# Retention followed by a squared-ReLU FFN: from chunk 10 on, one group of retention products per chunk, with the running state made one chunk ahead

## The chip, the cores and the metric

The kernel runs on one core of a Trainium2 chip. The metric is the device time of one execution in microseconds. A core has TensorE for matrix products (PE in the profile, and PEld for its weight loads), VectorE (DVE), ScalarE (ACT), GpSimd (POOL) and SyncE (SP), which here only issues DMAs. Each engine has its own instruction stream and takes it in order. Between engines, one waits for another by a semaphore.

## The reference, cut to what matters

```
# q, k, v: [8 batches, 8 heads, 576 positions, 64]
scores = q @ k.T / sqrt(64)
ret    = scores * where(i >= j, gamma_h ** (i - j), 0)      # gamma_h = 1 - 2**(-5-h)
attn   = ret @ v                                            # per batch and head
x      = attn.transpose(0, 2, 1, 3).reshape(4608, 512)      # tokens x model width
h      = maximum(x @ w_in, 0)                               # w_in  512 x 2048
out    = (h * h) @ w_out                                    # w_out 2048 x 512
```

The two FFN weights come as 64-bit floats and are turned into 32-bit floats on the chip.

## The kernel before, in words

**Retention.** A sequence of 576 positions is cut into chunks of 128 and a last one of 64: `ci` is 0 to 4 in a batch, and chunk 5b+4 is the half chunk. There are 40 chunks. Because the decay is a power, it can be split over q and v: GpSimd scales q (`scale_q`, L375) and v (L452, in `scores`) by tables, and the rest is linear attention. A chunk is worked in row halves of 64 positions. For each half there are three products per head:

- scores, k times q (L442, into `sc_ps`), which VectorE masks (L450) into `ret`;
- own, the half's v times its masked scores (L464, into `x_ps`);
- from the state, the running sum u of earlier k times v, times q (L499, also into `x_ps`).

A fourth, grow (L467, into `u_ps`), adds the half's k times v to the sum. ScalarE copies `u_ps` to one of three `u_sb` tiles (`grown`, L473), and `x_ps` to the FFN's input `xT` (L521).

All are products of 64x64 tiles. A product takes its contraction from 64 of the 128 rows of the array (a row half) and writes 64 of 128 output partitions (a column half), so four can stand in the array side by side. A product of 32-bit floats is two instructions in the trace. `own` has the row half of the position half h; `grow` is emitted beside it with the other row half; scores and products from the state take their row half from the head's parity `e`. Two products from different row halves that add to the same place of `x_ps` have to be kept apart: `retain_b` ends with a copy of two columns of `x_ps` by ScalarE (L502), and the products of `retain_c` wait for it.

**The FFN.** Blocks of 512 tokens are multiplied by a Strassen-like scheme of seven products a to g (`ffn_in`, L621, j = 0 to 6 below written a..g) for each of four groups `mp`. So a block takes 28 FFN steps of eight matmuls, into three rotating PSUM banks (`ps_f`). After product a ScalarE copies the bank (L631). After d ScalarE applies ReLU (L637) and GpSimd squares (L638). After the others VectorE adds, and squares (L628 and its neighbours). The first block goes another way (`first_in`, L585). A second phase, from about 560 us on, multiplies by `w_out` (L928) and has nothing of retention in it.

**The order.** It is written out by hand, and every engine's stream follows the program. In iteration i the loop emits for i > 4: `retain_a(i-1)` (own of half 1 beside grow of half 0, then `grown`), `ffn(i-1, 0)`, `retain_b(i-1)` (products from the state), `scores(i)`, `retain_c(i-1)` (own of half 0 beside grow of half 1, then the copy to `xT`), `ffn(i-1, 1)`. A half chunk has no `retain_a` products. I call each unbroken run of retention products on TensorE a visit: A for `retain_a`, BC for the rest. `ffn` emits as many FFN steps as a pacing table (`PACE`) allows for the tokens that have gone by, one to six a call. When a chunk crosses a block's border, `retain_c` first copies the part before the border, then emits FFN steps until block n-2 is finished (forced steps), and then copies the rest.

From chunk 11 on (`N_TURN`), q and k are transposed by VectorE in 32x32 tiles (`flip`, L395, two instructions a chunk) and ScalarE moves the tiles into place (`move`, L410: 16 copies for a full chunk, 8 for a half one). `ffn` takes some moves ahead of every step, and `move(C, i)` takes what is left of chunk i. The conversion of `w_out` goes in small items between the FFN steps (`w_out_parts`). One kind of item is VectorE's (L210, L214), and two activations of ScalarE (L218, L219) follow it. `held` keeps the items with ScalarE work out of the last two steps before a BC visit.

```
            retain_a(i - 1)
            if i < N_TURN:
                turn(i)
            move(C, i)
            ffn(i - 1, 0)
            retain_b(i - 1)
            if i < N_CH:
                scores(i)
            retain_c(i - 1)
            if N_TURN <= i + 2 < N_CH:
                flip(i + 2)
            ffn(i - 1, 1)
```

Of the kernel before, what the change touches and what calls it, by code (L numbers as in the profile page):

```python
# [9 lines left out]
F32 = mybir.dt.float32  # L10
# [5 lines left out]
C = 128  # L16
CH = C // 2
# [23 lines left out]
def kernel(  # L41
# [33 lines left out]
    nc = tc.nc  # L75
    ctx.enter_context(tc.manual_schedule())

    B, H, S, D = q.shape
# [242 lines left out]
            f and f()  # L321

    dv = only.tile([128, H, 2 * NCH], F32, name="dv")
    exp_bias = const.tile([128, 1], F32, name="exp_bias")
    nc.gpsimd.memset(exp_bias, -896.0 * 2.0 ** 23)
    idle, ident = (W[6][:, at:at + 128] for at in (2688, 2816))
# [30 lines left out]
    def rows(half, n=64):  # L357
        return slice(64 * half, 64 * half + n)
# [19 lines left out]


    N_TURN = 11  # L380
    moves = []

    def new_qk(i):
# [23 lines left out]
    def move(count, i=N_CH):  # L407

        while moves and count and moves[0][0] <= i and (moves[0][1] <= done[0] or count == C):
            nc.scalar.copy(*moves.pop(0)[2:])  # L410
# [16 lines left out]
    def scores(i):  # L427

        b_, ci, c0, cs = chunks[i]
        qT, kT = st[i]["qT"], st[i]["kT"]  # L430
# [6 lines left out]
        n_h = cs // CH  # L437
        for hp in range(HP):
            for h in range(n_h):
                for e in range(2):  # L440
                    t = slice(CH * h, CH * h + CH)
                    nc.tensor.matmul(sc[e][rows(h), hp, :], lhsT=kT[rows(e), hp, t], rhs=qT[rows(e), hp, t],  # L442
                                     start=True, stop=True, skip_group_check=True)

        r = st[i]["ret"] = st[i]["kT"].rearrange("p (e a) (b t) -> p e (a b) t", e=2, b=2)
        if i < N_EARLY:
            for e in range(2):
                nc.vector.tensor_tensor(r[:cs, e, :, :], sc[e][:cs], msk[:cs, 0, :, :].to_broadcast([cs, HP, CH]), op=ALU.mult)
        else:
            nc.vector.tensor_tensor(r[:cs], both[:cs], msk[:cs].to_broadcast([cs, 2, HP, CH]), op=ALU.mult)  # L450
        vs = st[i]["vs"] = loaded[i][2]
        nc.gpsimd.tensor_tensor(vs[:cs], vs[:cs],  # L452
                                dv[:cs, :, ci:ci + 1].to_broadcast([cs, H, D]), op=ALU.mult)
# [18 lines left out]
    def grown(i, h):  # L472
        nc.scalar.copy(u_sb[(2 * chunks[i][1] + h + 1) % 3], u_ps[0])  # L473
# [30 lines left out]
    def retain_c(i):  # L504

        b_, ci, c0, cs = chunks[i]
        own, grow = within(i, 0)
        more = ci + 1 < NCH
        for j in range(0, len(own), 2):
            for f in own[j:j + 2] + (grow[j:j + 2] if more else []):  # L510
                f()
        tok = b_ * S + c0
        at = tok
        p = xp[0][:, :, 0:256].rearrange("p a (g t) -> p a g t", g=2)
        while at < tok + cs:
            n = at // TOK

            while steps and steps[0][0] <= n - 2:
                step()
            end = min(tok + cs, (n + 1) * TOK)  # L520
            nc.scalar.copy(xT[n][:, :, at - n * TOK:end - n * TOK].rearrange("p (a g) t -> p a g t", a=2),  # L521
                           p[:, :, :, at - tok:end - tok])
            if more and at == tok:
                grown(i, 1)
# [4 lines left out]
        st[i] = loaded[i] = None  # L529

# [175 lines left out]
    def ffn(i, half):  # L706

        gone[0] += chunks[max(0, min(i, N_CH - 1))][3] / 2
        if steps and steps[0][0] == 0:

            move(6)
            for f in (step, lambda: convert(6)) if half else (lambda: convert(6), step):
                f()
            if half and steps and steps[0][0] == 0:
                step()
                convert(6)
            return
        if not behind:
            behind.append((gone[0] - HALF, done[0]))
        points = behind + [p for p in PACE if p[0] > behind[0][0]]  # L720
        want = points[-1][1]
        for (x0, y0), (x1, y1) in zip(points, points[1:]):
            if gone[0] < x1:
                want = y0 + (y1 - y0) * (gone[0] - x0) / (x1 - x0)
                break
        count = max(1, int(want) - done[0])
        while steps and count:
            held[0] = half == 0 and count <= 2

            move(4 if half and len(moves) > 8 else 3 if half else 2 if count > 1 else 0)  # L730
            busy[0] = len(flips) > 0
            for f in flips[:1]:
                f()
            del flips[:1]
            step()
            count -= 1
        held[0] = busy[0] = False
# [15 lines left out]
    for i in range(N_CH + 1):  # L753
        if i <= N_EARLY:

            if i == 1:
                convert(2)
            elif i == 2:
                convert(5)
            if i >= 1:  # L760
                retain_a(i - 1)
                if i < 3:
                    warm(4, False)
                elif i == N_EARLY:
                    turn(i)
                else:
                    convert(1)
                    first_in(1, (0,))
                    convert(5)
                retain_b(i - 1)  # L770
                if i < 3:
                    warm(4, False)
                retain_c(i - 1)
            convert((0, 1, 1, 0, 0)[i])
            if i == N_EARLY:
                fetch_raw(2)
                step()
            scores(i)
            if i == 2:
                convert(5)  # L780
                first_in(0, (0,))
            elif i == 3:
                convert(1)
                first_in(2, (0,))
                convert(3)
            elif i == N_EARLY:
                convert(3)
                step()
                convert(5)
            scale_q(i + 1, nc.gpsimd)  # L790
            if i < N_EARLY:
                if i < 2:
                    warm(6, False)
                if i + 1 < N_EARLY:
                    turn(i + 1)
        else:
            if i == N_EARLY + 1:
                gone[0] = TOK
# [6 lines that stand above are left out]
            if i < N_CH:  # L805
                scores(i)
            retain_c(i - 1)
            if N_TURN <= i + 2 < N_CH:
                flip(i + 2)
            ffn(i - 1, 1)  # L810
        if i == 0:
            fetch_raw(2)
        if i < N_TURN - 1:
            load(i + 3)
        else:
            if i == N_TURN - 1:
# [262 lines left out]
```

## Time and profile before

| what | us |
|---|---|
| three timed runs | 974.66, 974.70, 975.62 |
| their median | 974.7 |
| profiled execution: its span, first to last instruction | 974.5 |
| PE busy in it | 953.6 (98%) |
| DVE busy | 778.5 (80%) |
| ACT busy | 341.8 (35%) |
| POOL busy | 128.9 (13%) |
| stretch of the retention from chunk 10 on, 118.4 to 520.5 | 402.1 |
| in it: PE, DVE, ACT, POOL busy | 396.7, 334.7, 252.4, 94.3 |

The profiled execution has no other time than its span; it lies 0.2 us below the median of the timed runs. A busy PE is one with a product in flight, and products overlap, so that PE at 98% says that it seldom stood still, not that it worked at its peak. ScalarE's 35% is an average over the run: in the stretch of the retention it is 63%, and after it little. In an answer of the timeline a row is: start in us, duration, engine, line, operation, output<-inputs, shapes, how many were merged, and in brackets how long the engine had been idle and what it waited for.

### The profile page before, as it was taken

Reading aid. Unit: us, or ns where it says so; the run is one execution under the profiler, and the core shown is the slowest. Engines: PE = TensorE matmul, PEld = TensorE weight load, DVE = VectorE, ACT = ScalarE, POOL = GpSimd, SP = SyncE. Lnnn points to the kernel's source line nnn. Section 1 sums busy time; section 2 is a strip of 40 time slices with the busy share of each in tenths; the row PEclk is TensorE's granted clock in tenths of the full one; section 3 lists DMA queues with packets and bytes.
Section 4 is the critical chain, followed back from the end, with each engine's and each line's share of the span. In section 5 each row is a group of like instructions: output and inputs, shape, how many; then the busy total and the mean of one; then the engine's idle time right before and its main releaser. Section 6 shows DMA issues by size and latency. Waiting matters only on the chain.

```text
span 974.5 us, 24019 instructions
## 1 busy us (share of the span) xinstructions
PE 953.6 (98%) x10108; PEld 851.7 (87%) x10108; DVE 778.5 (80%) x1447; ACT 341.8 (35%) x848; POOL 128.9 (13%) x121
## 2 busy tenths in 40 slices
PE   6899999999999999999999999999999999999998
PEld 6645788888878888888888899999999999999998
DVE  3889799787797887888776587787888788787876
ACT  2554384864764857756631000000000000000000
POOL 3221223312222221222110000000000000000000
PEclk7999999999999999999999999999999999999999
DMA  9975756657738766487147986545353454524241
GB/s 203 245 205 160 186 161 164 184 168 242 217 93 262 207 192 188 121 279 211 62 166 274 396 309 249 191 157 184 109 205 141 160 198 171 208 100 173 88 174 44
DMA packets 172011, 181.43 MB, mean 186 GB/s; under 512 B 118144, under 2 KB 132480, under 8 KB 165248
## 3 DMA queue, kind: packets, MB, share of 16 engines
q1 hardware_dynamic: 169792, 179.38, 58.1%
q8 instruction: 79, 1.29, 0.6%
q10 hardware_dynamic: 2112, 0.52, 0.3%
q14 instruction: 28, 0.23, 0.1%
HBM read 109.36 MB, written 70.52 MB: 185 GB/s over the span
## 4 chain that ended last, share of the span: by engine, by line
PE 92%; DVE 3%; ACT 2%; DMA 2%; issue 1%; SPq 0%; DVEq 0%
PE h_b L621 17%; PE o_b L928 17%; PE h_a L621 11%; PE h_c L621 11%; PE o_a L928 11%; PE o_c L928 11%; PE h_ps L585 4%; PE x_ps L464 3%; PE x_ps L499 2%; PE sc_ps L442 2%; DMA g<-g_dram 1%; PE u_ps L467 1%; DVE w L225 1%; DVE w L228 1%; PE t_ps L421 0%
## 5 line engine op out<-in xcount | busy, mean ns | idle before, releaser
L621 PE MATMUL h_b<-room,w 128*128 128x256 f32 x768 | 185.7, 385 | 1.9 <-DVE room L548 1.9
L410 ACT COPY qk<-flip 32x256 f32<-32x256 f32 x416 | 167.4, 402 | 11.3 <-DVE flip L395 5.4
L621 PEld LDWEIGHTS h_b<-room,w 128*128 128x128 f32 x768 | 143.8, 190 | 22.9 <-issue 2.0
L928 PE MATMUL o_b<-w,room 128*128 128x128 f32 x1168 | 144.4, 275 | 0.2 <-DVE room L880 0.2
L928 PEld LDWEIGHTS o_b<-w,room 128*128 128x128 f32 x1168 | 137.3, 192 | 0.4 <-DVE room L880 0.4
L928 PE MATMUL o_c<-w,room 128*128 128x128 f32 x1008 | 123.0, 275 | 0.0
L621 PE MATMUL h_c<-room,w 128*128 128x256 f32 x512 | 122.8, 383 | 0.0
L621 PE MATMUL h_a<-room,w 128*128 128x256 f32 x512 | 122.5, 382 | 0.0
L928 PEld LDWEIGHTS o_c<-w,room 128*128 128x128 f32 x1008 | 117.7, 192 | 0.0
L942 ACT COPY r<-o_a 128x128 f32<-128x128 f32 x53 | 14.1, 265 | 272.3 <-PE o_a L928 236.6
L621 PEld LDWEIGHTS h_c<-room,w 128*128 128x128 f32 x512 | 97.0, 191 | 13.7
L621 PEld LDWEIGHTS h_a<-room,w 128*128 128x128 f32 x512 | 96.0, 190 | 13.9 <-issue 0.5
L928 PE MATMUL o_a<-w,a 128*128 128x128 f32 x688 | 85.6, 275 | 0.0
L928 PEld LDWEIGHTS o_a<-w,a 128*128 128x128 f32 x688 | 81.2, 192 | 0.1
L638 POOL TENSOR_TENSOR room<-room 128x512 f32<-128x512 f32 x32 | 35.0, 1094 | 347.0 <-ACT room L637 294.2
L628 DVE SCALAR_TENSOR_TENSOR room<-room 128x512 f32<-128x512 f32 x96 | 73.7, 767 | 3.3
L585 PE MATMUL h_ps<-room,w 128*128 128x512 f32 (+1 forms) x152 | 58.9, 535 | 2.9 <-DVE w L228 2.2
L640 DVE TENSOR_TENSOR room<-h_b,room 128x512 f32<-128x512 f32 x32 | 22.1, 690 | 49.5 <-PE h_b L621 49.5
L375 POOL TENSOR_TENSOR q_ld<-q_ld,dv 128x512 f32<-128x512 f32 (+1 forms) x39 | 45.9, 1177 | 83.5 <-DMA q_ld<-in_q_dram 65.2
L464 PEld LDWEIGHTS x_ps<-qk,v_ld 64*64 64x64 f32 x1152 | 40.3, 136 | 16.7 <-issue 13.2
L464 PE MATMUL x_ps<-qk,v_ld 64*64 64x64 f32 x1152 | 49.6, 226 | 4.0 <-ACT u_sb L502 2.0
L452 POOL TENSOR_TENSOR v_ld<-v_ld,dv 128x512 f32<-128x512 f32 (+1 forms) x40 | 48.9, 1224 | 12.6 <-DMA v_ld<-in_v_dram 12.6
(104 smaller groups left out, 1335.3 us busy)
## 6 DMA issues: line engine op xcount, KB each, us to landing
g_dram<-room SPq DMA_DIRECT2D x32, 1280.0 KB, 5.7
a<-g_dram SPq DMA_DIRECT2D x30, 1024.0 KB, 5.8
room<-g_dram SPq DMA_DIRECT2D x15, 1024.0 KB, 5.8
w<-w_dram SPq DMA_DIRECT2D x7, 1792.0 KB, 15.3
out_dram<-room SPq DMA_DIRECT2D x17, 512.0 KB, 3.3
w<-in_moe_w_in_dram SPq DMA_DIRECT2D x16, 512.0 KB, 5.3
w<-in_moe_w_out_dram SPq DMA_DIRECT2D x16, 512.0 KB, 4.3
v_ld<-in_v_dram SPq DMA_DIRECT2D x31, 256.0 KB, 4.0
```

Source lines behind the costliest of these rows:

```text
L375: engine.tensor_tensor(t, t, dv[:cs, :, NCH + ci:NCH + ci + 1].to_broadcast([cs, H, D]), op=ALU.mult)
L410: nc.scalar.copy(*moves.pop(0)[2:])
L442: nc.tensor.matmul(sc[e][rows(h), hp, :], lhsT=kT[rows(e), hp, t], rhs=qT[rows(e), hp, t], start=True, stop=True, skip_group_check=True)
L452: nc.gpsimd.tensor_tensor(vs[:cs], vs[:cs], dv[:cs, :, ci:ci + 1].to_broadcast([cs, H, D]), op=ALU.mult)
L464: own.append(lambda hp=hp, e=e, b=b: nc.tensor.matmul(x_at(hp, b, h), lhsT=s["vs"][rows(h), 2 * hp + b, :], rhs=s["ret"][rows(h), e, hp, : ...
L499: nc.tensor.matmul(x_at(hp, b, h), lhsT=u[rows(e), hp, :], rhs=s["qT"][rows(e), hp, CH * h:CH * h + CH], start=clears(b, hp // 2), stop=Fa ...
L585: nc.tensor.matmul(p.rearrange("p h t -> p (h t)"), lhsT=w[:, c, :], rhs=xT[0][:, c, lo * HT:hi * HT], start=(c == 0), stop=(c == N_DM - 1))
L621: nc.tensor.matmul(p[:, mm, :], lhsT=w[:, c, :], rhs=xs[n][right][:, c, :], start=(j in OPENS and mm == 0 and c == 0), stop=(j in CLOSES a ...
L628: nc.vector.scalar_tensor_tensor(t, t, 0.0, t, op0=ALU.max, op1=ALU.mult)
L638: nc.gpsimd.tensor_tensor(g["A11"], g["A11"], g["A11"], op=ALU.mult)
L640: nc.vector.tensor_tensor(g["A22"], p, p15, op=ALU.add)
L928: nc.tensor.matmul(p, lhsT=s["lefts"][left][:, m, :], rhs=w_out[j][:, m, WO_SLOT[right], :], start=(i in OPENS and m == 0), stop=(i in CLO ...
```

## The change

From iteration 11 on, the two visits of a chunk become one, `whole(i)`, and the two calls of `ffn` become one, `ffn(i-1, 2)`, whose token count is the second half of chunk i-1 and the first half of the next, so that the pacing at the `xT` copies is the same as before. `whole(i)` emits:

1. own of half 0 beside grow of half 1; after the first half of them a copy by ScalarE of one column of a small tile (`mark`), which waits for them (`f1`); then `grown(i, 1)`;
2. scores of chunk i+1, position half 0 only;
3. products from the state for both halves; their first waits for `f1`; after their last a second small copy (`f2`), for full chunks;
4. own of half 1 beside grow of half 0 of the next chunk, first half of them;
5. scores of chunk i+1, position half 1 only, and the mask;
6. the second half of step 4; own waits for `f2`;
7. the copies to `xT`, and `grown(i+1, 0)` after the first of them.

A half chunk has no own of half 1, and in the chunk before a half chunk step 5 has no products and there is no grow for the next chunk: a half chunk has only half 0, and its state goes no further. The state for a chunk's half 1 is thus made in the visit of the chunk before it. The scaling of v for chunk i+1 (`scale_v`) moves from `scores` to the end of iteration i, after `ffn(i-1, 2)` and just ahead of `whole(i)`, whose step 4 reads it. `ffn(., 2)` takes two to four moves a step, by how many are still due for the next chunk, none in its last step; and `held` covers the last step only. Iteration 10 keeps the old visits and adds grow of half 0 of chunk 10 after them.

```diff
+    N_ONE = N_TURN - 1
...
+    def scored(i, hs):
+        if hs == (0,):
+            scores(i, True)
+        for h in hs:
+            if h < chunks[i][3] // CH:
+                for hp in range(HP):
+                    score(i, st[i]["sc"][0], hp, h)
...
+        if i < N_ONE:
+            scale_v(i)
+
+    def scale_v(i):
+        ci, cs = chunks[i][1], chunks[i][3]
         vs = st[i]["vs"] = loaded[i][2]
         nc.gpsimd.tensor_tensor(vs[:cs], vs[:cs],
                                 dv[:cs, :, ci:ci + 1].to_broadcast([cs, H, D]), op=ALU.mult)
...
+    def seen(done_):
+        a = nc.scalar.copy(mark[:, 1:2], mark[:, 0:1])
+        after(a, done_)
+        return a
...
+    def whole(i):
...
+        out_of, into = own_of(i, 0), grow_of(i, 1) if more else []
+        f1 = seen(beside_each(out_of, into, (0, 2))[-1])
+        beside_each(out_of, into, (4, 6))
+        if more:
+            grown(i, 1)
+        if i + 1 < N_CH:
+            scored(i + 1, (0,))
+        f2 = None
+        for h in range(cs // CH):
+            if 2 * ci + h == 0:
+                continue
+            u = u_sb[(2 * ci + h) % 3]
+            for hp, e, b in HEADS[0:2] + HEADS[4:6] + HEADS[2:4] + HEADS[6:8]:
+                m = nc.tensor.matmul(x_at(hp, b, h), lhsT=u[rows(e), hp, :], rhs=s["qT"][rows(e), hp, CH * h:CH * h + CH],
+                                     start=clears(b, hp // 2), stop=False, skip_group_check=True)
+                if f1:
+                    after(m, f1)
+                    f1 = None
+        if cs == C:
+            f2 = seen(m)
+        grows = i + 1 < N_CH and chunks[i + 1][3] == C
+        out_of, into = own_of(i, 1) if cs == C else [], grow_of(i + 1, 0) if grows else []
+        beside_each(out_of, into, (0, 2))
+        if i + 1 < N_CH:
+            scored(i + 1, (1,))
+            masked(i + 1)
+        last = beside_each(out_of, into, (4, 6))
+        if f2:
+            after(last[0], f2)
+        x_out(i, lambda: grown(i + 1, 0) if grows else None)
...
         gone[0] += chunks[max(0, min(i, N_CH - 1))][3] / 2
+        if half == 2:
+            gone[0] += chunks[min(i + 1, N_CH - 1)][3] / 2
...
-            held[0] = half == 0 and count <= 2
-
-            move(4 if half and len(moves) > 8 else 3 if half else 2 if count > 1 else 0)
+            held[0] = half != 1 and count <= (1 if half else 2)
+
+            if half == 2:
+                due = sum(m[0] <= i + 2 for m in moves)
+                move(max(2, min(4, -(-due // (count - 1)))) if count > 1 else 0)
+            else:
+                move(4 if half and len(moves) > 8 else 3 if half else 2 if count > 1 else 0)
...
+        elif i > N_ONE:
+            move(C, i)
+            whole(i - 1)
+            if N_TURN <= i + 2 < N_CH:
+                flip(i + 2)
+            ffn(i - 1, 2)
...
+            if i == N_ONE:
+                for f in grow_of(i, 0):
+                    f()
+                grown(i, 0)
...
+            if i == N_ONE:
+                ffn(i, 0)
...
+        if N_ONE - 1 <= i < N_CH - 1:
+            scale_v(i + 1)
```

`beside_each(own, grow, js)` emits, for each j, two of the first list and then two of the second; `after` adds a semaphore wait.

More of the change, by code (lines that the diff above doesn't have):

```diff
@@ L323 @@
     dv = only.tile([128, H, 2 * NCH], F32, name="dv")
+    mark = const.tile([128, 2], F32, name="mark")
+    nc.vector.memset(mark, 0.0)
     exp_bias = const.tile([128, 1], F32, name="exp_bias")
@@ L425, in turn, with scores @@
         nc.vector.tensor_copy(to[:, 0].rearrange("p d h t -> p h d t"), p[:, :n_h, 0, :, :])
-    def scores(i):
+    def scores(i, halves=False):
         b_, ci, c0, cs = chunks[i]
-        qT, kT = st[i]["qT"], st[i]["kT"]
         if i < N_EARLY:
@@ L436, in scores, with score, masked @@
             sc = [both[:, e, :, :] for e in range(2)]
-        n_h = cs // CH
+        st[i]["sc"] = sc if i < N_EARLY else (sc, both)
+        if halves:
+            return
         for hp in range(HP):
[L439 to L443, printed above, removed]
+            for h in range(cs // CH):
+                score(i, sc, hp, h)
+        masked(i)
+    def score(i, sc, hp, h):
+        for e in range(2):
+            t = slice(CH * h, CH * h + CH)
+            nc.tensor.matmul(sc[e][rows(h), hp, :], lhsT=st[i]["kT"][rows(e), hp, t], rhs=st[i]["qT"][rows(e), hp, t],
+                             start=True, stop=True, skip_group_check=True)
+    def scored(i, hs):
[5 more added lines that the diff above has]
+                    score(i, st[i]["sc"][0], hp, h)
+    def masked(i):
+        b_, ci, c0, cs = chunks[i]
+        sc = st[i]["sc"]
+        if i >= N_EARLY:
+            sc, both = sc
         r = st[i]["ret"] = st[i]["kT"].rearrange("p (e a) (b t) -> p e (a b) t", e=2, b=2)
@@ L511, in retain_c, with x_out @@
                 f()
+        x_out(i, lambda: grown(i, 1) if more else None)
+    def x_out(i, after):
+        b_, ci, c0, cs = chunks[i]
         tok = b_ * S + c0
@@ L522, in retain_c @@
                            p[:, :, :, at - tok:end - tok])
-            if more and at == tok:
-                grown(i, 1)
+            if at == tok:
+                after()
             at = end
@@ L529, in retain_c, with grow_of @@
         st[i] = loaded[i] = None
+    HEADS_1 = [(hp, e, e if hp < HP // 2 else 1 - e) for e in (1, 0) for hp in (0, 2, 1, 3)]
+    def grow_of(i, h):
+        ci = chunks[i][1]
+        if ci == 0 and h == 0:
+            u_ps[0] = ps_u.tile([128, HP, D], F32, tag="u", name="u_ps")
+        u = u_ps[0]
+        return [lambda hp=hp, e=e, b=b: nc.tensor.matmul(
+            u[rows(e), hp, :], lhsT=loaded[i][1][rows(h), 2 * hp + e, :], rhs=st[i]["vs"][rows(h), 2 * hp + b, :],
+            start=(ci == 0 and h == 0 and hp == 0), stop=(hp == HP - 1), skip_group_check=True) for hp, e, b in HEADS]
@@ new lines, in own_of, with after @@
+    def own_of(i, h):
+        s = st[i]
+        return [lambda hp=hp, e=e, b=b: nc.tensor.matmul(
+            x_at(hp, b, h), lhsT=s["vs"][rows(h), 2 * hp + b, :], rhs=s["ret"][rows(h), e, hp, :],
+            start=clears(b, hp // 2), stop=False, skip_group_check=True) for hp, e, b in HEADS_1]
+    def after(later, earlier):
+        tc.add_manual_dep(later.ins, earlier.ins.name,
+                          mybir.DependencyInfo(mybir.DependencyClass.Sync, mybir.DependencyReason.DATA), reason="row halves")
@@ new lines, in seen, with beside_each @@
+    def seen(done_):
+        a = nc.scalar.copy(mark[:, 1:2], mark[:, 0:1])
+        after(a, done_)
+        return a
+    def beside_each(own, grow, js):
+        made = []
+        for j in js:
+            made.extend(f() for f in own[j:j + 2] + grow[j:j + 2])
+        return made
+    def whole(i):
+        b_, ci, c0, cs = chunks[i]
+        s = st[i]
+        xp[0] = ps_x.tile([128, 2, 256], F32, tag="x", name="x_ps", padded_shape=[128, 2, 512])
+        clean.clear()
+        more = ci + 1 < NCH
+        out_of, into = own_of(i, 0), grow_of(i, 1) if more else []
[6 more added lines that the diff above has]
+        f2 = None
+        for h in range(cs // CH):
+            if 2 * ci + h == 0:
[19 more added lines that the diff above has]
+        x_out(i, lambda: grown(i + 1, 0) if grows else None)
```

## The prediction, written before the result was known

> **What bounds the kernel now.** I read the page first, then the timeline around the visits, then the clock by windows. The page's chain of work that ended last:
>
> ```profile
> PE 92%; DVE 3%; ACT 2%; DMA 2%; issue 1%; SPq 0%; DVEq 0%
> ```
>
> TensorE sets the time; DMA adds 2%. So a change is worth what it adds to or takes from TensorE's stream. The timeline around an A visit gives its price:
>
> ```profile
> 302.33 1.89 PE L621 MATMUL h_b<-room,w 128*128 128x256 f32 x8
> 304.15 0.27 PE L464 MATMUL x_ps<-qk,v_ld 64*64 64x64 f32 x2
> ...
> 304.38 0.23 PE L464 MATMUL x_ps<-qk,v_ld 64*64 64x64 f32 x2
> 304.39 0.23 PE L467 MATMUL u_ps<-v_ld,k_ld 64*64 64x64 f32 x2
> 304.43 0.23 PE L464 MATMUL x_ps<-qk,v_ld 64*64 64x64 f32 x2
> ...
> 304.78 1.99 PE L621 MATMUL h_a<-room,w 128*128 128x256 f32 x8
> 306.61 0.38 PE L621 MATMUL h_b<-room,w 128*128 128x256 f32 x1
> ```
>
> From 302.33 to 306.61, 4.28 us, lie two FFN steps and the visit. Steps without a visit between follow at 1.73 us (306.61 and 308.33), so the visit costs 0.82. Its 32 instructions go in eight rounds of four; a round takes 0.058 us (304.32, .38, .43, .49): 0.47. The other 0.36 is the price of leaving the 128x128 products and coming back. I call it the switch.
>
> How many instructions fit in a round depends on which quarters of the array they use:
>
> ```profile
> 310.61 0.56 PEld L442 LDWEIGHTS sc_ps<-qk 64*64 64x64 f32 x16
> 319.09 0.56 PEld L442 LDWEIGHTS sc_ps<-qk 64*64 64x64 f32 x32
> 319.67 0.57 PEld L464 LDWEIGHTS x_ps<-qk,v_ld 64*64 64x64 f32 x16
> ```
>
> Scores of a full chunk take 32 instructions, of a half chunk 16, and both 0.56 us: scores of one position half only use one column half, two quarters, so a round holds two. The same with a half chunk's own without grow (L464, 16 in 0.57).
>
> The third view is a BC visit that starts at 205.44, after an FFN step d:
>
> ```profile
> 205.44 0.69 PE L499 MATMUL x_ps<-qk,u_sb 64*64 64x64 f32 x32
> 205.59 0.60 ACT L637 ACTIVATE room<-h_a 128x512 f32<-128x512 f32 x1 [3.09 <-issue]
> 206.20 0.16 ACT L502 COPY u_sb<-x_ps 128x2 f32<-128x2 f32 x1
> 206.27 1.04 POOL L638 TENSOR_TENSOR room<-room 128x512 f32<-128x512 f32 x1 [11.49 <-ACT room L637]
> 207.27 1.06 POOL L452 TENSOR_TENSOR v_ld<-v_ld,dv 128x512 f32<-128x512 f32 x1
> ```
>
> d's ReLU ends 0.75 us into the visit, GpSimd's square then runs, and the scaling of v ends 2.89 us into the visit. Now that is hidden: that v is first read some FFN steps later.
>
> **What the skill says.** The Trainium skill, "TensorEngine Tiling (Array Packing)", Key Properties: changing the tiling mode drains TensorE, and different tiles run in parallel. The trace agrees: 0.36 us a switch, 7 ns from one tile's start to the next's, 58 ns until the same tile's. Its Gotcha 1: row tiles may not access one PSUM bank at once and software must order them; hence `f1` and `f2`. "TensorE: Matmul & The Clock Gate", Architectural detail: ScalarE and GpSimd are strict FIFO; the trace agrees (L452 follows L638 at once). Same page, Part 1: an idle window of about 3.4 us halves TensorE's clock. The trace has one such, at clock 0.50:
>
> ```profile
> 287.49:290.91 3.42, 1.51 (x37) 1.28 (x37) 3.39 (x6) 2.57 (x6) 0.00 (x0) 1.00 0.00 0
> 290.91:294.32 3.41, 3.41 (x10) 2.66 (x9) 2.85 (x6) 0.00 (x0) 0.00 (x0) 0.50 0.21 29
> ```
>
> TensorE was busy for 1.51 of 3.42 us, then slow for a window.
>
> **The change, part by part** (30 visits, chunks 10 to 39).
>
> *Rounds and switches.* Before: ci=1, 2: A 0.82 (8 rounds) and BC 1.80 (24 rounds 1.40, switch 0.36, some 0.04 for L502): 2.62. ci=3: the same. ci=0: 0.82 and a BC of 20 rounds: 2.45. ci=4: BC alone, 20 rounds and a wait of 0.12: 1.65. After, the scores of a full next chunk come as two halves of 8 rounds each, where both together took 8. ci=1, 2: 8+8+8+8+8 = 40 rounds, 2.33+0.36 = 2.69 (+0.06). ci=0 has half the state products: 36 rounds, 2.46 (+0.01). ci=3: no second score half, but own of half 1 is alone, 8 rounds: 32 rounds, 2.22, and a wait for `f2`. The tiny copy's loop, from the half-chunk visits: product 0.218, 0.07 until the copy, 0.16, 0.055 until the next product: 0.50. Only own's first half, 0.23, covers it: 0.27 more, 2.50 (-0.13). ci=4: own alone 8, score halves 16, state 4, grow alone 8: 36 rounds, 2.46 (+0.81): it never had an A visit to lose. Chunk 39 saves 0.31; the grow added behind chunk 9 costs 0.47. Sum: 6x0.01+12x0.06-6x0.13+5x0.81-0.31+0.47 = +4.3 us. So 24 switches (8.6 us) go and 12.9 us of half-filled rounds come. Elsewhere 12 to 16 rounds (0.7 to 0.9) lie between a tiny copy's product and its waiter: hidden if ScalarE is free.
>
> *GpSimd.* `scale_v(i+1)` stands behind d's square and ahead of the visit that reads it. Step 4's grow comes after 24 rounds, 1.45 us in. Where d is the last FFN step before the visit, the row above says that v is ready at 2.89: TensorE waits 1.49, and all behind it in its queue too. I laid the FFN steps of each interval out by the pacing table; for the kernel before it gives the runs of steps seen in the trace. d stands last, with a grow to come, before visits 15, 16, 17, 19, 22, 26, 27, 35, 36, 37. In 27 and 36 ScalarE is later still (below). 7x1.49 + 1.72 (half chunk 19, whose grow comes after 20 rounds) = 12.1; visit 25 gives 1.4 more, because d's ReLU there is stuck behind moves: 13.5. With e last, the scaling ends about 1.15 in: hidden. Ends: 0 if something lets v be scaled earlier; 18 if GpSimd runs at its slow 1.5 us.
>
> *ScalarE.* A move takes 0.402. An interval after a border has forced steps without moves, then four steps with 4+4+4+0, and four are left to be flushed in front of the visit. The kernel before shows such an interval's start:
>
> ```profile
> 469.76 0.72 ACT L218 ACTIVATE w<-w,exp_bias 128x512 uint32<-128x512 uint32 x1 [5.93 <-DVE w L210]
> 470.39 0.66 ACT L219 ACTIVATE w<-w 128x512 f32<-128x512 uint32 x1
> 470.95 0.35 ACT L521 COPY room<-x_ps 128x256 f32<-128x256 f32 x1
> 471.32 1.65 ACT L410 COPY qk<-flip 32x256 f32<-32x256 f32 x4
> 472.99 0.58 ACT L631 COPY room<-h_a 128x512 f32<-128x512 f32 x1
> ```
>
> The FFN run began at 463.07, so L631 ends at +10.5. Two times four moves, d's ReLU, four moves and `f1` bring 16.2, while TensorE wants it at 7 steps (12.4) + 0.98 = 13.35: visit 27 loses 2.9. Visit 36, without a conversion item, loses 1.5. Visit 24 (two flushed, a conversion two steps before) 0.85, visit 25 0.4, some 0.5 elsewhere: 6.2. Ends: 2, and 10 if conversion items stand right before more visits.
>
> *VectorE.* The stall at 288 (a block's sums late) loses its cover, an A visit: +0.8. The later mask is read a whole interval on: nothing, hidden by six FFN steps; without them its 0.68.
>
> *What goes.* Waits now seen: A visits at 229.7 and 471.4 behind that late L521 (0.88, 1.22; now seven FFN steps lie between), the late L502 at 180.3 (1.03), 343.9 (0.35), smaller ones 0.2: -3.7.
>
> SP's loads and the squares keep their number and order. Tiny copies: 0.16 each, in ScalarE's slack.
>
> Sum: +4.3+13.5+6.2+0.8-3.7 = +21.1. The profiled execution's 974.5 becomes 995.6; the median stood 0.2 above: 995.8.
>
> **Rivals.** (1) *Nothing is late.* GpSimd and ScalarE deliver before TensorE asks, v by 1.45 us into each visit and `f1` by 0.98. Then 19.7 falls away: 976.1, no measurable change. It decides where all lateness together stays under 0.5 us. For it: with a, b, c, f or g last, GpSimd is done early. Against: the 2.89 of the third view, met with nothing before it in GpSimd's queue. (2) *Half of it*: only one of the two queues is late, or d stands last less often: 982 to 989. (3) *The clock.* Each long stall may cost a window at half clock: 3.41 us at half speed loses 1.7. 0.44 busy tripped it; the stall at 471 (2.25 of 3.40 busy) didn't. Visits with 1.5 us of waiting stay near 0.55. If half of ten trip, and VectorE, which waits longer for scores, falls behind: 1002 to 1015. (4) *Half-filled rounds pack with their neighbours* and (1) holds as well: 974.5-8.6-3.7+0.8 = 963. Against: score halves stand between products that are in order with them.
>
> **How the numbers follow.** A measurement of this kernel can tell 0.2% (1.95 us) from no change. The likeliest case, 0.55, gives 995.8, by itself 989 to 1002. (2) 0.16, (3) 0.13, (1) 0.14 with its spread over 971 to 981: faster 0.05, same 0.05, slower 0.04. (4) 0.02, faster. So faster 0.07, same 0.05, slower 0.88. The range 979 to 1008 leaves out (4), most of (1) and half of (3).
>
> **What would show it.** Visits of 2.69 us without waits, and score halves of 16 instructions in 0.47 us each: the rounds. Grow (L467's successor) waiting for v about 1.5 us in eight visits behind d: GpSimd. Long waits for ScalarE at visits 27 and 36, with moves ahead of the tiny copy. The A stalls of 229 and 471 gone. The prediction is wrong if grow doesn't wait, or if score halves take 0.23.

## The result, and the profile after

The changed kernel takes 1007.9 us (median of four runs, 1006.8 to 1009.1) against 974.7 in the same session: a ratio of 1.034, 95% interval 1.0326 to 1.0355. It is 33.2 us slower; 21.1 were predicted. The profiled execution spans 1005.7 us against 974.5. Lines have moved: in the new listing own is L577, grow L571, the products from the state L616, scores L450, the tiny copies L586, the scaling of v L479, the moves L413, an FFN product L724.

The page after, busy time by engine, the chain that ended last, and two groups:

```profile
PE 967.6 (96%) x10108; PEld 869.9 (86%) x10108; DVE 777.5 (77%) x1448; ACT 344.9 (34%) x872; POOL 129.1 (13%) x121
...
PE 39%; DVE 1%; issue 0%; DVEq 0%
...
L472 DVE TENSOR_TENSOR qk<-sc_ps,msk 128x512 f32<-128x512 f32 (+1 forms) x36 | 24.6, 685 | 46.4 <-PE sc_ps L450 46.4
...
L571 PE MATMUL u_ps<-v_ld,k_ld 64*64 64x64 f32 x768 | 41.7, 229 | 12.1 <-POOL v_ld L479 12.1
```

PE was busy 953.6 us before and is busy 967.6 now; the other 17 of the 31 us are time in which nothing was in flight, so more than half of the loss is waiting. The last line names a wait that the kernel before did not have: grow waits 12.1 us for GpSimd's scaling of v. VectorE's mask waits 46.4 us for scores, but that is slack of VectorE: its result is wanted a whole interval later. The chain covers only the second phase this time (39% of the span) and says nothing of the retention.

Where the 31 us lie is read from the timeline, visit by visit: the time between the last FFN product before a visit and the first after it, against visits without a wait. The retention's stretch grew by 34.3 us (the part before it was some 2 us shorter in this execution):

| in the stretch of the retention | predicted | measured |
|---|---|---|
| rounds and switches | +4.3 | +4.7 |
| grow waits for GpSimd, in nine visits | +13.5 | +14.0 |
| waits for ScalarE, and what else is in the visits | +6.2 | +9.9 |
| FFN steps: sums of block 4 | +0.8 | +0.4 |
| FFN steps: k of chunk 13 arrives late | 0 | +4.0 |
| half-clock windows: four instead of one | 0 | +5.1 |
| waits of before that are gone | -3.7 | -3.9 |
| sum | +21.1 | +34.2 |

The timeline after, around visit 16, which starts at 210.24 behind an FFN step d, to be held against the third view of before:

```profile
210.24 0.27 PE L577 MATMUL x_ps<-qk,v_ld 64*64 64x64 f32 x2
...
210.40 0.60 ACT L740 ACTIVATE room<-h_a 128x512 f32<-128x512 f32 x1 [2.98 <-issue]
...
210.76 0.63 PE L450 MATMUL sc_ps<-qk 64*64 64x64 f32 x16
...
211.07 1.07 POOL L741 TENSOR_TENSOR room<-room 128x512 f32<-128x512 f32 x1 [13.23 <-ACT room L740]
...
212.10 1.05 POOL L479 TENSOR_TENSOR v_ld<-v_ld,dv 128x512 f32<-128x512 f32 x1
...
213.21 0.27 PE L571 MATMUL u_ps<-v_ld,k_ld 64*64 64x64 f32 x2 [1.13 <-POOL v_ld L479]
...
214.28 1.99 PE L724 MATMUL h_b<-room,w 128*128 128x256 f32 x8
```

ReLU, square, scaling, grow: the chain of the prediction. The scaling ends 2.91 us into the visit (2.89 predicted). From one product's start to the next (from start to start, below) TensorE loses 1.35 us here; over the nine visits it is 1.32 to 2.55, together 14.0.

The timeline after in front of visit 27, which starts at 377.37: ScalarE's queue and the product that waits for it.

```profile
374.81 0.59 ACT L734 COPY room<-h_a 128x512 f32<-128x512 f32 x1
375.42 3.33 ACT L413 COPY qk<-flip 32x256 f32<-32x256 f32 x8
...
378.77 0.60 ACT L740 ACTIVATE room<-h_a 128x512 f32<-128x512 f32 x1
379.39 1.64 ACT L413 COPY qk<-flip 32x256 f32<-32x256 f32 x4
...
381.05 0.19 ACT L586 COPY mark<-mark 128x1 f32<-128x1 f32 x1
...
381.30 0.74 PE L616 MATMUL x_ps<-qk,u_sb 64*64 64x64 f32 x32 [2.77 <-ACT mark L586]
```

Eight moves, d's ReLU, four moves, the tiny copy: the order the prediction wrote out, and 2.99 us lost from start to start for 2.9 forecast.

Two things were not in the sum. The clock, by windows after (us from the start, length, busy time and instructions of PE, PEld, DVE, ACT, POOL, then the granted clock, the DMA share, GB/s):

```profile
344.27:347.68 3.41, 1.32 (x64) 1.17 (x56) 2.65 (x3) 1.13 (x4) 2.86 (x2) 1.00 0.00 0
347.68:351.09 3.41, 3.17 (x47) 2.88 (x48) 1.31 (x2) 1.30 (x4) 1.20 (x2) 0.50 0.71 209
378.40:381.81 3.41, 0.64 (x38) 0.52 (x36) 0.03 (x1) 3.01 (x8) 2.37 (x3) 1.00 1.02 294
381.81:385.23 3.42, 3.42 (x65) 3.03 (x57) 1.31 (x2) 1.64 (x5) 0.70 (x1) 0.50 0.90 197
```

These are visits 25 and 27. After a window in which the waits left TensorE 1.32 or 0.64 us of 3.41 busy, the next runs at half clock. The windows from 262.35 and 491.04 run at half clock too, after windows with 1.91 and 1.66 us busy. Four windows that lose 1.7 us each, against one before, make +5.1.

And the loads, in the timeline after (SPq is SP issuing a DMA):

```profile
123.48 0.38 SPq L666 DMA_DIRECT2D g_dram<-room  x1
123.91 0.52 SPq L148 DMA_DIRECT2D q_ld<-in_q_dram  x1
...
127.05 0.56 SPq L148 DMA_DIRECT2D k_ld<-in_k_dram  x1
...
132.80 0.71 DVE L398 STREAM_TRANSPOSE flip<-k_ld 128x512 f32<-128x512 f32 x1 [6.19 <-DMA k_ld<-in_k_dram]
...
134.14 1.99 PE L724 MATMUL h_c<-room,w 128*128 128x256 f32 x8 [2.74 <-DVE room L738]
...
136.81 1.99 PE L724 MATMUL h_b<-room,w 128*128 128x256 f32 x8 [0.67 <-DVE room L743]
```

SP reaches the loads at 123.91, behind a store of the FFN's output that it could only issue when the data was there. VectorE's flip waits 6.19 us for the k that arrives too late, the FFN's sums stand behind the flip, and TensorE stands twice, 3.1 and 1.1 us from start to start where 0.22 is usual. With the slower start after each, the way from visit 10 to visit 11 takes 18.6 us, against 14.7 in the kernel of the second experiment below: 4.0 us. In the kernel before, the same loads go out first and the store after them:

```profile
115.97 0.39 SPq L148 DMA_DIRECT2D q_ld<-in_q_dram  x1
...
117.47 0.47 SPq L148 DMA_DIRECT2D k_ld<-in_k_dram  x1
...
127.10 0.37 SPq L563 DMA_DIRECT2D g_dram<-room  x1
```

### The profile page after: what moved, and what is told of

Its sections match the earlier page's. It is cut to its first block, busy times and chain, and to the rows that moved or that the text cites. A ratio compares the mean times of both kernels' runs of the same rounds, so it can differ in the third digit from the quotient of the medians.

```text
span 1005.7 us, 24074 instructions
## 1 busy us (share of the span) xinstructions
PE 967.6 (96%) x10108; PEld 869.9 (86%) x10108; DVE 777.5 (77%) x1448; ACT 344.9 (34%) x872; POOL 129.1 (13%) x121
## 5 line engine op out<-in xcount | busy, mean ns | idle before, releaser
L724 PE MATMUL h_b<-room,w 128*128 128x256 f32 x768 | 186.8, 387 | 2.7 <-DVE room L651 1.9
L413 ACT COPY qk<-flip 32x256 f32<-32x256 f32 x416 | 167.3, 402 | 5.5
L724 PEld LDWEIGHTS h_b<-room,w 128*128 128x128 f32 x768 | 146.8, 193 | 24.9 <-issue 2.2
L724 PE MATMUL h_c<-room,w 128*128 128x256 f32 x512 | 122.5, 382 | 2.7 <-DVE room L738 2.7
L724 PE MATMUL h_a<-room,w 128*128 128x256 f32 x512 | 122.0, 381 | 0.0
L724 PEld LDWEIGHTS h_c<-room,w 128*128 128x128 f32 x512 | 97.2, 191 | 16.7 <-DVE room L738 3.1
L724 PEld LDWEIGHTS h_a<-room,w 128*128 128x128 f32 x512 | 96.5, 190 | 14.0 <-issue 0.5
L731 DVE SCALAR_TENSOR_TENSOR room<-room 128x512 f32<-128x512 f32 x96 | 69.5, 724 | 3.3
L377 POOL TENSOR_TENSOR q_ld<-q_ld,dv 128x512 f32<-128x512 f32 (+1 forms) x39 | 49.0, 1258 | 100.1 <-DMA q_ld<-in_q_dram 85.9
L472 DVE TENSOR_TENSOR qk<-sc_ps,msk 128x512 f32<-128x512 f32 (+1 forms) x36 | 24.6, 685 | 46.4 <-PE sc_ps L450 46.4
L571 PE MATMUL u_ps<-v_ld,k_ld 64*64 64x64 f32 x768 | 41.7, 229 | 12.1 <-POOL v_ld L479 12.1
L688 PEld LDWEIGHTS h_ps<-room,w 128*128 128x128 f32 x152 | 27.6, 190 | 25.7 <-issue 21.9
```

The costliest lines, as they stand in the source:

```text
L377: engine.tensor_tensor(t, t, dv[:cs, :, NCH + ci:NCH + ci + 1].to_broadcast([cs, H, D]), op=ALU.mult)
L571: return [lambda hp=hp, e=e, b=b: nc.tensor.matmul(u[rows(e), hp, :], lhsT=loaded[i][1][rows(h), 2 * hp + e, :], rhs=st[i]["vs"][rows(h), ...
L688: nc.tensor.matmul(p.rearrange("p h t -> p (h t)"), lhsT=w[:, c, :], rhs=xT[0][:, c, lo * HT:hi * HT], start=(c == 0), stop=(c == N_DM - 1))
L724: nc.tensor.matmul(p[:, mm, :], lhsT=w[:, c, :], rhs=xs[n][right][:, c, :], start=(j in OPENS and mm == 0 and c == 0), stop=(j in CLOSES a ...
L731: nc.vector.scalar_tensor_tensor(t, t, 0.0, t, op0=ALU.max, op1=ALU.mult)
```

## The experiments

### The scaling of v taken out of the square's way

```diff
             whole(i - 1)
+            if i < N_CH - 1:
+                scale_v(i + 1)
...
-        if N_ONE - 1 <= i < N_CH - 1:
+        if N_ONE - 1 <= i <= N_ONE:
             scale_v(i + 1)
```

> The kernel after, with the scaling of v for chunk i+1 issued right after the visit of chunk i-1 instead of right before the visit of chunk i. Theory of the GpSimd queue: the nine waits of grow for v (13.7 us of gaps) vanish; three of the four windows at half clock followed such a wait (262, 348, 491 us), so up to 5 us more goes; ScalarE's waits at the same visits come out from behind them and stay. 1007.9 becomes about 990 (987 to 995). Rival, the waits come from the v loads or from GpSimd being slow: within 3 us of 1007.9. Rival, the clock has nothing to do with the waits: about 994, four slow windows remain.

Measured: 990.2 us (ratio 1.0164, interval 1.0144 to 1.0183), 17.7 less than the changed kernel. GpSimd's timeline in it:

```profile
199.62 1.06 POOL L479 TENSOR_TENSOR v_ld<-v_ld,dv 128x512 f32<-128x512 f32 x1
212.31 1.06 POOL L741 TENSOR_TENSOR room<-room 128x512 f32<-128x512 f32 x1 [11.63 <-ACT room L740]
```

v for the visit that starts at 211.5 is scaled eleven us ahead; the square at 212.31 has nothing of the retention behind it, and no grow waits for GpSimd in the whole trace. Visits behind d that wait for nothing else take 2.5 to 2.8 us. The waits for ScalarE at visits 27 (2.99) and 36 (1.75) stand as they were, so these are two independent causes, and GpSimd's is the larger: 14.0 of the 17.7 us are its waits. The windows at half clock behind them are gone, but this execution still had three in the stretch, behind the late loads, visit 13 and visit 27, so that the other 3.7 us are not traced to the clock. One wait grew: that of visit 20 for ScalarE, from 0.38 to 1.63 us.

### The loads back in front

```diff
             ffn(i - 1, 1)
-            if i == N_ONE:
-                ffn(i, 0)
...
+        if i == N_ONE:
+            ffn(i, 0)
```

The second place is behind the loads of the same iteration; nothing but SP's order changes.

> The kernel after, with the one moved call of ffn in iteration 10 put behind the loads of chunks 13 and 14 as it was before; only the order of SyncE's stream changes. Theory of the load queue: the transpose of chunk 13 no longer waits 6.2 us for its k, the two stalls in the FFN run at 124 to 140 us (3.95 us) vanish: about 1004. Rival, VectorE was late by itself there: no change.

Measured: 1004.8 us (1.0308, 1.0284 to 1.0331), 3.1 less. Its timeline:

```profile
116.00 0.47 SPq L148 DMA_DIRECT2D k_ld<-in_k_dram  x1
...
123.95 0.38 SPq L666 DMA_DIRECT2D g_dram<-room  x1
...
126.86 0.70 DVE L398 STREAM_TRANSPOSE flip<-k_ld 128x512 f32<-128x512 f32 x1
```

The loads go out ahead of the store, the flip finds its data, and of the 4.0 us of FFN stall nothing is left; the 3.1 gained agree with it within the interval.

### Moves in the forced steps

```diff
             while steps and steps[0][0] <= n - 2:
+                if i >= N_ONE:
+                    move(4)
                 step()
```

> The kernel after, with four moves ahead of each forced step at a block's border, so that nothing is flushed in front of visits 27 and 36. Theory of the ScalarE queue: the waits for the tiny copy at these two visits (3.0 and 1.75 us) and the window at half clock behind visit 27 (1.7 us) go, about 1001.5 to 1003. At visit 36 less may show, 1.5 us of GpSimd's lateness comes out from behind ScalarE's, so 1002 to 1005. Rival, moves don't matter and the conversion items hold ScalarE: no change.

Measured: 1004.2 us (1.0307, 1.0289 to 1.0324), 3.7 less. The tiny copies of visits 27 and 36 are no longer waited for. But grow in both visits now waits 1.50 us for v: both visits stand behind a d, and GpSimd's lateness had been hidden behind ScalarE's. A stall removed shows the next one, and only the difference is gained, 1.7 us; one half-clock window less (three for four in the stretch) gives about as much again.

### All three together

> The kernel after with the three edits together: v scaled right after the previous visit, the loads of chunks 13 and 14 ahead of the moved FFN steps, four moves ahead of each forced step. Theory that the waits are those of three queues and add up: 990.2 less 3 to 4 for the loads, less 4.7 for visits 27 and 36, less 1.7 to 3.4 for windows at half clock: 979 to 983. What is left over 974.4 is then rounds (4.7), the conversion item before visit 13 (1.5), waits for the tiny copy elsewhere. Rival, one wait only hides the next and they don't add: 986 or more.

Measured: 982.0 us (1.0085, 1.0068 to 1.0102), 25.9 less than the changed kernel, where the three alone give 17.7 + 3.1 + 3.7 = 24.5. The clock of its profiled execution:

```profile
core 0: 977.6 us, clock 1.000
```

In this execution no window of the retention falls to half clock: the +5.1 hang on the waits. It was the fastest of the four, 979.7 us; the others took 981.2 to 984.3 at mean clocks of 0.998, 0.996 and 0.991, and no trace shows where their half-clock windows lie. So what is left of the loss, 7.6 us by the medians, is the rounds (stall-free visits still take 2.67 us), single waits at visits 13 and 20 (1.4 each), 24 (0.7) and 35 (0.6), and a part of the clock that is not shown.

### Half-filled rounds put into the kernel before

```diff
-        for hp in range(HP):
-            for h in range(n_h):
+        for hp, h in [(hp, h) for hp in range(HP) for h in range(n_h)] if i <= N_TURN - 1 else [(hp, h) for h in range(n_h) for hp in range(HP)]:
+            for _ in range(1):
```

The kernel before with the scores of half 0 ahead of those of half 1, and nothing else.

> The kernel before, with the scores of chunks 11 to 39 in the order of the changed kernel (all heads of position half 0, then all of half 1); nothing else. 23 of these chunks are full. Theory of the half-filled rounds: 8 rounds of 0.058 us more for each, 0.47 us, 10.7 us in all, less some 0.04 us a visit in which the copy that orders row halves was waited for: 974.7 becomes 984 to 985.5. Rival, two halves pack with their neighbours: 974.7.

Measured: 977.9 us against 974.4 (1.0035, 1.0021 to 1.005): 3.5 us, a third of the forecast. The expectation failed, and the timeline of this kernel shows how; the same two rows in the kernel before follow.

```profile
410.26 0.77 PE L442 MATMUL sc_ps<-qk 64*64 64x64 f32 x26
410.81 0.27 PE L464 MATMUL x_ps<-qk,v_ld 64*64 64x64 f32 x1
410.86 0.28 PE L442 MATMUL sc_ps<-qk 64*64 64x64 f32 x3
```

```profile
281.06 0.65 PE L442 MATMUL sc_ps<-qk 64*64 64x64 f32 x32
281.53 0.27 PE L464 MATMUL x_ps<-qk,v_ld 64*64 64x64 f32 x2
```

Mixed, 32 scores take 0.47 us to the next product. Half behind half they should take 0.94; own's first product starts 0.55 in, with scores still starting after it. Half-filled rounds that stand next to each other overlap, with each other and with the products behind them, and a visit of ci=1, 2 grows by 0.25 us and one of ci=0 or 4 by 0.14 to 0.20, not by 0.47. In the changed kernel the halves stand apart, and there stall-free visits took 2.67 us where 2.69 was forecast.

### Scores split by heads instead of by halves

```diff
-        for h in hs:
-            if h < chunks[i][3] // CH:
-                for hp in range(HP):
-                    score(i, st[i]["sc"][0], hp, h)
+        for hp in (0, 1) if hs == (0,) else (2, 3):
+            for h in range(chunks[i][3] // CH):
+                score(i, st[i]["sc"][0], hp, h)
```

The same products as in the kernel with all three edits, but each of the two places now holds both position halves of two head pairs, so that a full chunk's rounds are full.

> As the run with the three edits, and the scores of the next chunk divided between their two places by head pairs instead of position halves, so that each place has all four quarters: 4 rounds in each place where there were 8. Theory of the half-filled rounds: a full visit with a full next chunk falls from 2.57 us between FFN products to about 2.10 and some 0.05 to 0.25 of waiting for the tiny copies, whose cover falls from 12 rounds to 8: 24 visits by 0.25 to 0.45, 6 to 11 us, so 970 to 976. Rival, from the run with the kernel before: TensorE overlaps half-filled rounds anyway, and 2 us or less is gained.

Measured: 978.0 us (1.0035, 1.0022 to 1.0047), 4.0 less: short of the forecast of 6 to 11, and more than the rival's 2. Stall-free visits of full chunks fall from 2.67 to 2.47 us. But eight rounds instead of twelve now lie between a tiny copy's product and its waiter, and where a or d is the last FFN step the copy comes late: in some twelve visits. There the products behind it start 0.31 us after those ahead of it instead of 0.12, and 0.2 of the gain is given back.

### Conversion items held back

```diff
-            held[0] = half != 1 and count <= (1 if half else 2)
+            held[0] = half != 1 and count <= 2
```

and, to make up for it, a pace of 1.0 instead of 0.92 and a catch-up step at j = 1.

> As the run before in this list, and conversion items with ScalarE work held out of the last two FFN steps before a visit, as the kernel before does, with the pacing of these items quickened from 0.92 to 1.0 a step so that they end in time. Theory: the wait at visit 13 (1.5 us) and small ones at 11 and 20 go, 1 to 3 us less than the run before in this list. Rival: the quicker items crowd VectorE and it is no faster.

Measured: 975.2 us against 974.4 (1.001, 1.0003 to 1.0018): all but even with the kernel before. Visits 13 and 24 lost their waits, visit 20 did not. The hold and the pace were changed together; what each gives is not shown.

### The sums of block 4, in the old kernel and in the new

Both kernels stop for 1.9 to 2.0 us in front of product b of block 4 because VectorE makes a flip and other work before the block's second sum; in the prediction's view of the clock it is the window at 287.49. The edit makes that sum right behind the first and lets the flip wait for one step:

```diff
             sums_x[n + 1].pop(0)()
+            if j == 5 and len(sums_x[n + 1]) > 2:
+                sums_x[n + 1].pop(0)()
+                late_x[0] = True
```

> The kernel before with only the second sum of a late block moved ahead of the flip, as a control for the two others: the wait of 1.9 us before product b of block 4 and its half-clock window (1.7) go, 974.4 less 3.6 is 970.8, within 970 to 972.5. If it lands there, the part of the gain of the other two that comes from this edit has nothing to do with one group of products per chunk. If the window doesn't go with the wait, 972.5.

Measured: 971.9 us against 974.5 (0.9969, 0.996 to 0.9979). The stretch around the same step, in windows:

```profile
284.00:287.41 3.41, 3.41 (x17) 3.00 (x16) 3.38 (x6) 2.25 (x6) 0.32 (x1) 1.00 0.00 0
287.41:290.82 3.41, 3.41 (x46) 2.75 (x45) 3.34 (x6) 0.96 (x2) 0.00 (x0) 1.00 0.00 0
```

No wait and no window at half clock behind it. This is the fastest kernel of the study, and it has none of the change.

> The five edits as before it, and in the last FFN steps of a block whose successor's x came late, VectorE makes the second of the block's sums (T2, which product b of the next block reads) right behind the first and ahead of a flip, and whatever is left of the weight conversion is emitted before block 7's last group. Theory: TensorE's wait of 2.0 to 2.4 us in front of product b of block 4 and the half-clock window behind it (1.7) go: 975.2 less 3.7 is 971.5, within 970.5 to 973. Rival: product g's sum, now one instruction later, holds b's bank, and 0.9 of the wait stays with the half-clock window gone: 972.5. Rival: the wait goes but the window comes elsewhere, as in all runs but one so far: 973.

Measured: 975.7 us (1.0012, 1.0003 to 1.0021), no gain. The stall at 288 went, but this kernel lacked the catch-up step at j = 1, so seven items of the weight conversion were left and were emitted at once before block 7's last group:

```profile
533.94 0.69 DVE L745 TENSOR_TENSOR room<-h_b,room 128x512 f32<-128x512 f32 x1 [6.91 <-DMA g_dram<-room]
...
534.69 2.48 PE L726 MATMUL h_b<-room,w 128*128 128x256 f32 x8 [3.21 <-DVE room L745]
```

VectorE waits there for a store of the FFN's output to land, and TensorE for VectorE. How the left-over items make that store late was not traced; the wait is gone in the kernel with the catch-up step (two runs below).

The next run is this kernel with the items held out of three steps instead of two.

> The same with the conversion items with ScalarE work kept out of the last three steps before a visit instead of two. Theory: the moves of chunk 21 no longer stand behind an item that waits 2.6 us for VectorE, and visit 20 falls from 4.0 to 2.35 us: 1.6 less than the kernel without this edit, 969.9 if that gives 971.5. Rival: the items bunch up in fewer steps, their VectorE parts delay block sums and masks elsewhere, and nothing is gained: equal within 0.5 us.

Measured: 987.6 us (1.0132, 1.0115 to 1.0149). With still more of the conversion left to the end TensorE waits there for 5 and then 7 us. Visit 20 takes 2.3 us, but so it does in the run just before, without this edit: in both, the lagging conversion puts no item in front of visit 20. So this run tells nothing of its question.

> The kernel with the five edits (catch-up steps of the weight conversion included, which the kernel before this one lacked) and the second block sum ahead of the flip; nothing of the conversion is left to be emitted in one go. In the kernel before this one that rest made TensorE wait 3.4 us at 534.7 and cost a half-clock window (1.7). Theory: both go, and 975.7 less 5.1 gives 970.6, within 969.5 to 972.5. Rival: visit 20, which fell from 4.0 to 2.2 us there only because the conversion lagged, is slow again: 972.3 or more.

Measured: 973.4 us against 974.3 (0.9996, 0.9986 to 1.0006): not to be told from the kernel before, and above the forecast. The rest's stall is gone, and the rival was right that visit 20 is slow again once the conversion keeps up, as the timeline shows:

```profile
259.93 0.72 ACT L218 ACTIVATE w<-w,exp_bias 128x512 uint32<-128x512 uint32 x1 [2.36 <-DVE w L210]
...
261.26 1.24 ACT L413 COPY qk<-flip 32x256 f32<-32x256 f32 x3
...
261.71 0.33 PE L450 MATMUL sc_ps<-qk 64*64 64x64 f32 x2 [0.58 <-ACT qk L413]
```

ScalarE stands 2.36 us at a conversion item for VectorE, the last moves of chunk 21 stand behind it, and the scores wait for them.

The last run splits the scores three head pairs to one:

```diff
-        for hp in (0, 1) if hs == (0,) else (2, 3):
+        for hp in (0, 1, 2) if hs == (0,) else (3,):
```

> The same with the scores of three head pairs in the first place and of one in the second, so that twelve rounds instead of eight lie between the tiny copy's product and its waiter. Theory: the wait of 0.31 us for the tiny copy in some twelve visits behind a or d falls to 0.1, and own's second tiny copy, now covered by 0.46 us against its 0.50, adds 0.04 to twenty visits: 1.7 less than the kernel beside it, 968.9 if that gives 970.6. Rival: the copies are late because ScalarE is, not by cover, and nothing changes: equal within 0.5.

Measured: 973.5 us (0.9993, 0.9984 to 1.0003), no gain. The step to the first waiting product falls from 0.31 to 0.19 us in the visits behind a or d, and own's second half, behind the other tiny copy, rises from 0.12 to 0.23: what one copy gains in cover the other loses. Visits of full chunks behind a or d stay at 2.67 us.

## Why the prediction was right, and where not

*Direction, and most of the amount.* Slower by 21.1 was forecast, 33.2 came. That is 0.1 us inside the upper end of the range given, 979 to 1008, and outside the 989 to 1002 of the likeliest case by itself. The range reached so far because it took in half of rival (3), while 4.0 us of what filled it, the late loads, stood in no rival: that it held is in part luck. The three large terms hold. Rounds and switches: +4.3 forecast (the line as written adds up to 4.2), +4.7 measured; in visit 12 the scores of half 0 start two every 0.058 us, 0.47 in all, as said. GpSimd: the nine visits named are the nine that wait, 13.5 against 14.0, and with the scaling moved the waits are gone; here two errors cancel, visit 25 lost 2.55 for 1.4 and the other eight 11.5 for 12.1. ScalarE: visits 27 and 36 lost 2.99 and 1.75 us for 2.9 and 1.5. Rivals (1) and (2) fall with that, (4) with the stall-free visits; the waits said to go went (3.9 for 3.7).

*The clock: the step that failed most.* Rival (3) had the mechanism and its price, but the sum took only the likeliest case and set it at zero, on the ground that visits with 1.5 us of waiting stay near 0.55 busy. Neither part of that ground held. The working itself gave visit 27 a loss of 2.9 us; and 0.55 was not known to be safe, only that 0.44 tripped the clock and 0.66 did not. Here windows busy for 1.91 and 1.66 of 3.41 us, 0.56 and 0.49, tripped it. Nor need a window be idle, as in the sentence that the prediction cites: one that is partly idle is enough. The Trainium skill, "TensorE: Matmul & The Clock Gate", Part 1, says that the window of 3413 ns runs freely, and the trace agrees: the starts of the four half-clock windows lie 25, 10 and 32 times 3.413 us apart. So it matters where a wait falls on that grid. The stall behind the late loads shows it: in the changed kernel a border of the grid splits it, 2.17 and 1.91 us busy on the two sides, and no half clock follows; in the first and third experiments the same stall leaves one window with 0.84 and 0.86 us busy, and it does. Of the twelve visits that wait for more than one us, four paid. Three are those that waited longest, 27 (2.99 us), 25 (2.55) and 35 (0.63 and 1.56), and they paid in each of the traces of the changed kernel and the first three experiments in which these waits stand. Visit 19 (1.71) paid here and not in the second experiment, visit 13 (1.58) there and not here. So the size of a wait counts first, and near 1.6 us the grid.

*SP's loads: a wrong statement.* "SP's loads and the squares keep their number and order" was wrong: the FFN steps of chunk 10's first half had been moved ahead of the loads of iteration 10, and with them the store that SP issues for the FFN. The diff showed it (`if i == N_ONE: ffn(i, 0)`); the working had followed the moved step's VectorE and ScalarE work, not its DMAs. +4.0 us, 3.1 of it regained by undoing that one move.

*ScalarE elsewhere: a term sized too small.* The 0.5 for other visits became some 3: visit 13 (1.58), where a conversion item waited 4.25 us for VectorE, then 35 (0.63), 20 (0.38) and 17 (0.36). That is the upper end named, where conversion items stand right before more visits; the sum had taken the middle. About 1.5 us more of that row lies in the visits that wait for GpSimd, which take some 0.2 us longer than their wait explains; why is open.

*What the structure is worth.* With whole rounds, stall-free visits save 0.15 to 0.17 us in each of 24 chunks with two visits before and cost 0.43 in each of five half chunks: 24 x 0.16 - 5 x 0.43 = 1.7 us gained. The 0.2 that the exposed tiny copies take back in twelve visits is 2.4, more than all of it. A visit of 32 full rounds and one switch should take 2.23 us, and took 2.47. The other 0.24 are the tiny copies again: at each of the two the trace has a step of 0.12 and then one of 0.09 us where 0.04 is usual, 0.13 a copy. No run here leaves the copies out. No version of it tried here beat the old order with its one stall mended.

## What to carry to other kernels

Joining two groups of products saves a switch, but moves every input's deadline forward by an interval: for each input, write down which engine makes it and what that engine has in its queue ahead of it at that moment. For a step that is moved, do this for its DMAs also. Add up the waits last, against windows of the clock, since a wait of 1.6 us can cost 3.3.

## What the hardware showed that was not expected

- Half-clock windows lie on a fixed grid of 3.413 us. Of the windows on this grid from 120 us on that ran at full clock, those with up to 1.50 us of busy time were all followed by half clock, and those above 2.2 never. In between it isn't busy time alone. In the changed kernel 1.91 us busy with 67 mostly small products, at visit 19, tripped it, and 1.91 us busy with eight FFN products, at the late loads, did not; 1.54 to 1.55 us of FFN products, at the stall before b of block 4, did not in five kernels. Among windows of mostly small products, 1.66 to 2.11 us tripped it eight times and 1.88 to 2.08 did not six times. What is counted stays open.
- Products of 64x64 tiles that leave half of the array free overlap with what stands beside them in the queue: 0.25 us a visit where 0.47 was counted.
